# Turning the fourth batch's q and k by transposing transfers, spreading a bias by a matrix product, and a new order for the whole program

## The chip, the core and the metric

The kernel runs on one core of a Trainium2 chip. Five engines work side by side, each through its own list of instructions in order: PE (TensorE, matrix products; PEld is its loading of the stationary operand), DVE (VectorE), ACT (ScalarE), POOL (GpSimd) and SP (SyncE, which here only issues transfers). They wait for each other through semaphores. Transfers are issued from the lists of SP, ACT and POOL and are carried out by 16 DMA engines; SP's also do transposing transfers from SBUF to SBUF. The metric is the device time of one execution in microseconds (us), as a median over runs.

## What is computed

Cosine attention over 8 batches, 12 heads, 448 positions and a head dimension of 64, followed by a highway layer over all 3584 positions of width 768:

```python
q_n = q / (norm(q, axis=-1) + 1e-06)
k_n = k / (norm(k, axis=-1) + 1e-06)
scores = q_n @ k_n.T / tau                      # tau = 0.1
attn = softmax(scores)
x = (attn @ v), laid out as [8 * 448, 12 * 64]
H = maximum(x @ w_h, 0.0)
T = 1.0 / (1.0 + exp(-(x @ w_t + b_t)))
out = T * H + (1.0 - T) * x
```

## The kernel before

**Tiling.** Heads are worked on in pairs (head p and head p + 6), six pairs a batch, 48 steps s = 6 b + p in all. 448 positions are three chunks of 128 ("rows") and a tail of 64; the tails of a batch are handled together. Everything that goes into a matrix product is fp16; loads from DRAM convert on the way where POOL issues them.

**Stages of a batch b.** `load_main` and `load_v` (POOL's list) bring q, k, v rows into `qr`, `kr`, `vr`; `load_tails` (SP's list; for batch 0 k's on ACT's) brings the tails into `qt`, `kt`, `vt`. `square`, `tail_squares` and `folds` form the sums of squares (tile names `sq`, `f`, `n`), `newton` the reciprocal roots (`rs`). `scaled` multiplies rows by them into `qn`, `qtnorm` and `ktnorm` the tails into `kb`. Then q and k must be turned, the head dimension onto the partitions:

- `turn` (L565 on) and `turn_tails` (L594 on), for batches not in `BY_DMA`, on PE: seven 128x128 transposes a pair (L582 for six pieces of `qn`, L585 for the k tail in `kb`) into a PSUM tile `pB`, then one copy to `qT` on DVE or ACT (the line is that of the helper `copied`, L261); and three transposes of the batch's q tails (L607) with a copy to `tT` on DVE (L611).
- For batches in `BY_DMA`, `turn` issues one transposing transfer `qT<-qn` a pair (L572), and `turn_tails` one, `tT<-kb`, a batch (L599), both from SP's list.

`scores` makes the products of scores (L642 for the rows, four products a chunk on 64 rows of the array; L657 for the tail keys, on the whole array), each followed by an exponential on ACT (`E`, L648; `Et`, L661). `attend` multiplies by v on PE (L690, L694, L710; the appended column of ones in `vp` gives the sums) and DVE normalizes (`rd` L718, `x` L720). `ffn` takes a batch in four pieces g = 4 b + i: `x` is turned into `xT` (a transfer at L757 for batches 1 to 6, PE at L763 else), then products with `wt` and `wh` (L807 on 64 rows, L791 on 64 columns, L779 for the last piece), tanh on ACT (`tt`), and the gate on DVE and POOL (`hm` L867 and L879, `tt` L872, `os` L884), and stores from SP.

**The bias.** Up to piece 23 the bias enters as one more product: a row of ones times the bias, `pS<-bth,ones`, at the start of an accumulation. `bth` holds the bias in rows 0 and 64, zero elsewhere, loaded by two transfers (L375, POOL) after DVE has cleared it. From piece 24 (`ADDED`), that is from batch 6, DVE adds the bias from a tile `bias` that holds it on every partition (L837, L839). `bias` is filled by one broadcasting transfer from DRAM (L377, POOL).

**What sets the order.** The functions only write down 1717 operations, each with its engine and what it reads and writes. A table `ORDER` gives the order in which they are issued, and so the order of every engine's list; `SLOTS` says which buffer of its ring every tile gets (three PSUM tiles `pS` of two banks each, two `pB` of one, rings of two to four in SBUF); `MOVED` lists the operations that go to their second engine (`pick`); `URGENT` lists POOL operations that the next DVE operation must wait for. Nothing is decided at run time. At the start PE multiplies a constant tile with itself 40 times (`warm`, L310).

Of the kernel before, what the change touches and what calls it, by code (L numbers as in the profile page):

```python
# [20 lines left out]
18 17 2 3 5 0 78 20 19 33 83 21 6 23 11 4 84 24 29 22 77 1 16 8 74 87 28 75 42 25 36 81 40 9 43 27 26 35 32 44  # L21
278 45 31 46 276 7 47 30 56 48 49 274 51 57 50 13 54 34 55 58 10 59 65 52 60 94 76 61 99 72 273 14 53 62 98 100
63 64 95 117 488 90 118 101 82 93 487 91 105 66 489 103 106 107 92 277 96 104 67 119 275 68 137 120 281 136 15
490 69 279 97 108 138 283 122 70 71 300 38 139 128 280 175 129 39 145 194 86 146 12 193 126 37 491 89 156 127
109 174 88 1108 155 110 176 123 143 121 177 157 102 492 73 159 158 195 282 124 144 196 113 197 114 284 112 125
111 164 115 288 160 116 165 141 185 299 79 186 80 285 142 162 287 147 130 301 148 133 131 161 286 85 289 166
132 163 179 134 181 290 135 167 183 140 291 184 302 694 150 292 149 293 151 180 294 152 295 168 296 170 297 182
169 153 298 154 171 311 198 172 202 200 199 173 178 204 318 190 203 187 313 189 188 205 319 201 191 314 312 192
315 507 695 337 320 506 209 206 497 207 321 208 338 210 496 329 211 360 323 327 303 357 339 330 340 324 316 228
356 212 229 328 342 213 344 493 348 343 379 358 508 346 345 359 322 219 304 347 509 907 220 498 325 501 363 305  # L30
221 499 326 317 222 349 306 510 495 331 341 502 332 333 307 494 364 334 308 503 351 309 699 223 352 504 353 350
417 365 505 235 310 366 375 236 335 354 376 361 355 214 362 336 414 215 500 377 398 367 394 378 216 395 217 368
511 902 512 396 413 218 372 397 369 371 513 370 405 514 515 237 516 373 406 403 517 374 238 602 404 384 239 415
519 385 244 382 245 545 380 230 383 416 901 231 525 381 401 704 424 402 386 518 232 224 387 233 544 425 418 520
399 234 521 388 906 529 522 390 419 389 713 546 696 391 714 400 1109 246 392 547 526 393 697 420 247 225 905
422 421 527 601 408 703 528 407 582 409 410 698 603 548 423 564 532 604 248 533 411 553 563 412 249 554 583 536
428 226 427 537 429 426 250 555 430 620 251 431 556 534 523 252 432 535 715 530 260 584 531 705 549 903 253 261
585 524 551 716 565 700 552 706 539 566 540 538 550 1101 541 256 570 542 254 921 543 572 240 559 255 560 573
558 557 574 571 257 433 621 709 434 241 575 606 707 568 258 435 607 561 717 436 569 438 708 439 259 910 710 447
904 920 440 437 702 711 441 712 242 586 448 911 442 452 449 718 567 831 243 453 719 624 720 701 450 721 562 812  # L40
454 451 722 589 605 455 723 590 724 593 733 461 622 594 922 591 587 623 456 579 726 578 577 588 612 725 1102
262 613 752 265 592 443 1107 790 263 912 1110 266 576 727 728 264 267 608 580 916 610 581 751 462 1106 609 729
463 732 611 444 753 734 771 627 735 770 625 464 628 754 465 808 915 772 626 457 596 773 809 597 595 466 598 755
631 458 741 632 756 789 629 757 616 599 268 615 600 828 617 630 614 781 923 1302 476 782 445 742 479 917 477
924 1111 918 480 731 919 737 618 736 827 633 619 634 738 636 635 913 791 478 481 637 638 760 467 761 792 459
639 739 468 914 740 775 810 446 776 730 743 1301 469 811 460 744 758 269 470 908 759 270 762 1104 747 925 471
774 746 745 763 668 777 926 796 779 778 927 472 767 928 764 929 765 780 1112 748 654 977 1121 930 482 640 749
931 750 933 1120 655 766 1113 829 797 993 227 641 830 939 909 656 768 798 473 657 1105 799 957 642 769 995 643
658 938 645 644 956 940 646 1122 815 794 647 816 992 958 648 932 795 813 649 793 800 784 975 801 785 1103 786
814 783 483 994 838 484 836 839 834 659 1123 837 974 805 1303 804 787 1310 835 803 976 802 788 660 934 806 832  # L50
817 807 661 833 1029 935 662 818 474 819 663 843 1304 841 820 842 1114 840 1311 485 823 937 824 475 821 650 822
844 1320 1010 845 271 683 825 1136 686 826 1115 1011 1116 687 1124 846 684 1028 948 685 688 966 936 1030 946
651 669 947 1213 670 1321 1012 674 1117 1312 942 675 943 652 671 272 672 1306 1013 676 959 673 664 1305 677
1118 978 875 847 678 1505 979 848 679 960 1119 1511 852 486 1322 961 849 1323 1506 853 967 665 944 1315 850
1125 666 945 854 855 851 680 861 1126 856 941 862 949 1313 980 962 681 863 981 864 1127 1159 964 865 1128 951
1316 953 1002 1129 965 950 1130 952 1131 689 866 963 954 1324 1133 867 1003 982 1138 996 868 983 1139 869 955
# [116 lines left out]
def kernel(  # L173
# [11 lines left out]
    nc = tc.nc  # L185
# [824 lines left out]
```

## Time and profile before

| | us |
|---|---|
| median of 3 runs (lowest, highest) | 269.06 (268.74, 270.12) |
| the profiled execution, first to last instruction | 270.4 |
| busy: PE, DVE, ACT, POOL | 244.4, 228.5, 206.0, 115.9 |

The profile has no other time of the profiled execution than its span, and that lies 1.3 us over the median and 0.3 over the slowest run. Busy times are read with care: a PE product is shown from its start to a modelled end, and the products behind it start before that, so the starts tell how fast PE goes. Idle time in front of an instruction is put down to what ended it ("<-"). An answer cut into stretches gives the busy time of each engine in each; a share of DMA over 1 means that packets overlap.

### The profile page before, as it was taken

The numbers are of one execution on the slowest core, as the hardware profiler recorded it, in microseconds if no ns is written. First come the engines' busy times: TensorE is split into PE (matmuls) and PEld (weight loads), VectorE is DVE, ScalarE is ACT, GpSimd is POOL, SyncE is SP. The second block draws the span as 40 slices with busy tenths as digits, with TensorE's granted clock in tenths as the row PEclk, the third lists the DMA queues.
The fourth block names the chain that finished last, engine by engine and source line by source line (L and its number), as shares of the span: only waits on it lengthen the run. The fifth ranks groups of instructions, "written<-read, shape, count | busy, mean of one in ns | idle before, by whom it ended". The sixth has DMA issues, their size and how long they took to land.

```text
span 270.4 us, 9033 instructions
## 1 busy us (share of the span) xinstructions
PE 244.4 (90%) x3755; PEld 165.0 (61%) x3755; DVE 228.5 (85%) x513; ACT 206.0 (76%) x279; POOL 115.9 (43%) x151
## 2 busy tenths in 40 slices
PE   7088978999999999999899799997999999999991
PEld 3044666676776676667466557664767667767650
DVE  6599899999999898998976978997987864569894
ACT  3379999799999989989589499867868797961120
POOL 8757458563455649335450626314404522002140
PEclk9659999999999999999999799999999999999998
DMA  7999999999899797999999976999939949413133
GB/s 136 207 192 183 179 200 211 194 184 193 136 136 252 103 152 84 172 253 157 178 166 173 187 196 128 206 136 154 235 107 175 183 72 238 80 58 119 63 100 132
DMA packets 104025, 43.32 MB, mean 160 GB/s; under 512 B 97584, under 2 KB 101040, under 8 KB 103984
## 3 DMA queue, kind: packets, MB, share of 16 engines
q0 software_dynamic: 38608, 16.52, 49.1%
q1 hardware_dynamic: 63920, 25.50, 48.8%
q10 hardware_dynamic: 1456, 0.72, 1.0%
q8 instruction: 29, 0.48, 0.7%
q14 instruction: 12, 0.10, 0.1%
HBM read 38.21 MB, written 11.01 MB: 182 GB/s over the span
## 4 chain that ended last, share of the span: by engine, by line
PE 62%; DVE 20%; DMA 7%; issue 4%; ACT 3%; POOL 2%; SPq 1%; DVEq 0%; PEldq 0%; ACTq 0%; POOLq 0%
PE pS L807 26%; PE pS L642 9%; PE pB L694 8%; PE pS L791 4%; PE pB L710 4%; PE pB L657 3%; PE pB L690 3%; DMA kt<-in_k_dram 3%; DVE qn L258 3%; PE pB L582 2%; DMA qr<-in_q_dram 2%; DVE x L720 2%; DMA qT<-qn 2%; DVE f L421 2%; DVE hm L867 1%
## 5 line engine op out<-in xcount | busy, mean ns | idle before, releaser
L648 ACT ACTIVATE E<-pS 128x896 f16<-128x896 f32 x144 | 127.3, 924 | 26.2 <-PE pS L642 22.5
L807 PEld LDWEIGHTS <-xT 64*128 64x128 f16 x1128 | 53.8, 94 | 31.6 <-issue 2.6
L807 PE MATMUL pS<-wt,xT 64*128 64x384 f16 x576 | 56.6, 325 | 0.2 <-PEq L800 0.2
L807 PE MATMUL pS<-wh,xT 64*128 64x384 f16 x552 | 55.7, 323 | 0.2 <-DVE hm L867 0.2
L642 PE MATMUL pS<-qT 64*128 64x384 f16 x288 | 43.9, 332 | 2.3 <-DMA qT<-qn 1.8
L694 PE MATMUL pB<-vp,E 128*128 128x65 f16 x864 | 43.8, 194 | 0.0
L694 PEld LDWEIGHTS <-E 128*128 128x128 f16 x864 | 38.8, 98 | 2.6 <-issue 2.5
L867 DVE SCALAR_TENSOR_TENSOR hm<-pS,x 128x768 f16<-128x768 f32 (+1 forms) x33 | 27.3, 831 | 10.7 <-ACT tt L848 5.7
L642 PEld LDWEIGHTS <-qT 64*128 64x128 f16 x576 | 22.9, 95 | 19.6 <-issue 4.4
L690 PE MATMUL pB<-vp,Et 128*128 128x130 f16 x144 | 32.0, 222 | 2.3 <-DVE x L720 1.9
L258 POOL TENSOR_TENSOR qn<-kr,rs 128x384 f16<-128x384 f16 x24 | 19.8, 827 | 32.9 <-issue 10.0
L884 POOL TENSOR_TENSOR os<-x,hm 128x768 f32<-128x768 f16 (+1 forms) x11 | 15.8, 1441 | 37.7 <-DVE hm L879 17.3
L720 DVE SCALAR_TENSOR_TENSOR x<-pB,rd 128x448 f16<-128x448 f32 x48 | 29.7, 621 | 1.1
L661 ACT ACTIVATE Et<-pB 128x512 f16<-128x512 f32 x48 | 28.9, 609 | 0.9 <-PE pB L657 0.8
L642 PE MATMUL pS<-tT,qT 64*128 64x64 f16 x282 | 27.6, 190 | 0.0
L258 POOL TENSOR_TENSOR qn<-qr,rs 128x384 f16<-128x384 f16 x17 | 14.4, 850 | 14.0 <-DMA qT<-qn 5.6
L884 DVE TENSOR_TENSOR os<-x,hm 128x768 f32<-128x768 f16 (+1 forms) x22 | 18.5, 842 | 0.8 <-POOL os L884 0.6
L845 ACT ACTIVATE tt<-os 128x768 f16<-128x768 f32 (+1 forms) x8 | 6.1, 764 | 17.1 <-DVE os L839 10.0
L710 PE MATMUL pB<-vp,E 128*128 128x65 f16 x288 | 18.6, 195 | 0.5 <-POOL vp L261 0.5
L258 DVE TENSOR_TENSOR qn<-qr,rs 128x384 f16<-128x384 f16 x30 | 17.2, 577 | 0.5 <-POOL qn L258 0.4
L690 PEld LDWEIGHTS <-Et 128*128 128x128 f16 x144 | 14.1, 98 | 5.5 <-issue 4.3
L879 DVE TENSOR_TENSOR hm<-tt,hm 128x768 f16<-128x768 f16 (+1 forms) x33 | 16.4, 503 | 0.4
(116 smaller groups left out, 451.2 us busy)
## 6 DMA issues: line engine op xcount, KB each, us to landing
out_dram<-os SPq DMA_DIRECT2D x23, 384.0 KB, 3.0
vr<-in_v_dram POOLq DMA_DIRECT2D x8, 576.0 KB, 11.3
kr<-in_k_dram POOLq DMA_DIRECT2D x7, 576.0 KB, 10.8
qr<-in_q_dram POOLq DMA_DIRECT2D x7, 576.0 KB, 10.7
qt<-in_q_dram SPq DMA_DIRECT2D x16, 96.0 KB, 5.4
vt<-in_v_dram SPq DMA_DIRECT2D x16, 96.0 KB, 5.6
out_dram<-os SPq DMA_DIRECT2D x15, 96.0 KB, 2.7
kt<-in_k_dram SPq DMA_DIRECT2D x14, 96.0 KB, 6.7
```

The costliest lines, as they stand in the source:

```text
L258: return (nc.vector if eng == "DVE" else nc.gpsimd).tensor_mul(out_, a, c)
L642: ins = nc.tensor.matmul(dst, lhsT=qT[ln, 384 + 128 * c : 512 + 128 * c], rhs=rhs, start=True, stop=True)
L648: return nc.scalar.activation(R("E", s)[:, c, :, 0:448], R("S", 3 * s + c)[:, :, 0:448], AF.Exp, scale=inv_tau)
L661: op("ACT", f"expt {s}", lambda: nc.scalar.activation(R("Et", s)[:, 64:576], R("B", ("S", s))[:, :], AF.Exp, scale=inv_tau), key + 3, r=[( ...
L690: nc.tensor.matmul(U[:, 2 * c : 2 * c + 2, :].rearrange("p g e -> p (g e)"), lhsT=Et[:, 128 + 128 * c : 256 + 128 * c], rhs=vp[:, 6:8, :]. ...
L694: ins = nc.tensor.matmul(U[:, 2 * c + ab, :], lhsT=EF[:, j, 576 * ab + 128 * c : 576 * ab + 128 * c + 128], rhs=vp[:, 3 * ab + j, :], star ...
L710: ins = nc.tensor.matmul(U[:, 6, :], lhsT=lt, rhs=rh, start=(n == 0), stop=(n == 7))
L720: op("DVE", f"ev {s}", lambda: nc.vector.scalar_tensor_tensor(out=R("x", b)[:, :, D * p : D * p + D], in0=U_()[:, :, 0:D], scalar=0.0, in1 ...
L807: ins = nc.tensor.matmul(P[:, h, 0:MH], lhsT=lt, rhs=rh, start=(part == 0 and cc == (-1 if wi == 0 and not added else 0)), stop=(part == 1 ...
L867: return nc.vector.scalar_tensor_tensor(out=o_, in0=i0, scalar=0.0, in1=xs, op0=ALU.max, op1=ALU.subtract)
L879: op("DVE", f"gg{'h' if tail or last_ else ''} {nm}", lambda cs=cs: nc.vector.tensor_mul(R("hm", g)[:, cs], R("tt", g)[:, cs], R("hm", g)[ ...
L884: op(en, f"out{'h' if tail or last_ else ''} {nm}", lambda eng=eng, cs=cs: eng.tensor_add(R("os", g)[:, cs], xall()[:, cs], R("hm", g)[:, ...
```

## The change

Four things change together.

1. `BY_DMA` takes in batch 3. Its six turns on PE with their six copies, and the turn of its tails with a copy, become seven transposing transfers in SP's list.
2. The bias tile is no longer loaded by a broadcast. Two products `pS<-bth,ones` (`spread`, L380 of the new file) put the bias on all partitions of a PSUM tile, and one copy brings it to `bias`, on DVE or ACT; `MOVED` puts it on ACT.
3. `ORDER`, `SLOTS`, `MOVED` and `URGENT` are new from the first entry to the last. 104 operations change between DVE and POOL (54 to POOL, 50 to DVE), 25 between DVE and ACT (12 to ACT, 13 to DVE), 7 between ACT and POOL. `URGENT` has 37 entries in place of 50.
4. There are 1711 operations in place of 1717.

```diff
-18 17 2 3 5 0 78 20 19 33 83 21 6 23 11 4 84 24 29 22 77 1 16 8 74 87 28 75 42 25 36 81 40 9 43 27 26 35 32 44
...
+21 18 6 16 27 40 26 17 8 20 29 25 24 19 1 44 0 39 43 3 5 4 2 45 46 47 48 49 50 7 51 54 28 55 52 53 56 22 23 32
...
-    BY_DMA = (4, 5, 6, 7)
+    BY_DMA = (3, 4, 5, 6, 7)
...
-        op("POOL", "ld bb", lambda: nc.gpsimd.dma_start(bias[:, :], moe_b_t.partition_broadcast(128)), key + 30, w=[("bias", 0)])
+
+        def spread():
+            for h in range(2):
+                ln = slice(64 * h, 64 * h + 64)
+                ins = nc.tensor.matmul(R("S", ("bb", 0))[:, h, 0:MH], lhsT=ones[ln, 0:128], rhs=bth[ln, MH * h : MH * h + MH],
+                                       start=True, stop=True)
+            return ins
+
+        op("PE", "bbm", spread, key + 30, mode="T", r=[("zb", 0), ("bth", 0)], w=[("S", ("bb", 0))])
+        eng = pick("DVE", "ACT")
+        op(eng, "bbc", lambda eng=eng: copied(eng, bias.rearrange("p (h m) -> p h m", h=2), R("S", ("bb", 0))[:, :, 0:MH]), key + 30,
+           r=[("S", ("bb", 0))], w=[("bias", 0)])
```

Lines of the new file are one lower than the old ones up to L374, and ten higher behind the bias.

Three places of the new order. The first is ACT at the start of the program, before (`first` is the first pair's rows, `first_sq`, `first_n` and `first_rs` its squares, sums and roots; a number behind a name is the buffer):

```order
L264 ACTIVATE sq_89<-qt_76 128x384
L264 ACTIVATE sq_89<-qr_70 128x2x2x192
L264 ACTIVATE sq_90<-kr_73 128x2x3x192
L454 ACTIVATE rs_98<-n_96,tiny 128x36
L456 ACTIVATE rs_98<-rs_98 128x36
L264 ACTIVATE sq_90<-qr_70 128x2x3x192
L261 COPY qT_105<-pB_135 128x896
L648 ACTIVATE E_108<-pS_131 128x2x448
```

and now:

```order
L263 ACTIVATE sq_89<-qr_71 128x2x2x192
L263 ACTIVATE sq_89<-qt_77 128x384
L263 ACTIVATE sq_89<-kt_79 128x384
L260 COPY qT_106<-pB_134 128x896
L260 CAST bias<-pS_133 128x768
L464 ACTIVATE rs_100<-n_96,tiny 128x36
L466 ACTIVATE rs_100<-rs_100 128x36
L263 ACTIVATE sq_89<-kr_75 128x2x3x192
L263 ACTIVATE sq_89<-qr_71 128x2x3x192
L671 ACTIVATE Et_112<-pB_134 128x512
L658 ACTIVATE E_110<-pS_131 128x2x448
```

The first turn's copy has moved ahead of the roots and of the squares of pairs 3 to 5; the square of a k tail and the copy of the bias are new on ACT here.

The second is DVE at the start, from the sum of the first pair's squares to the copy of its turned q tail (`first_kb` is its k tail, `first_qtn` its q tail), before:

```order
L502 TENSOR_REDUCE first_n<-first_fb 128x15
L258 TENSOR_TENSOR sq_89<-kr_73 128x2x2x192
L506 TENSOR_TENSOR qn_101<-first,first_rs 128x2x3x64 x2
L516 TENSOR_TENSOR first_kb<-first_t,first_rs 64x64
L258 TENSOR_TENSOR sq_89<-kt_78 128x384
L421 TENSOR_TENSOR f_92<-sq_89 128x1152
L511 TENSOR_TENSOR first_qtn<-first_t,first_rs 128x128
L425 TENSOR_TENSOR f_94<-f_92 128x576
L427 TENSOR_REDUCE n_96<-f_94 128x36
L281 MEMSET Et_112 128x32 x2
L516 TENSOR_TENSOR first_kb<-first_t,first_rs 64x64
```

and now:

```order
L512 TENSOR_REDUCE first_n<-first_fb 128x15
L280 MEMSET first_kb 64x32 x2
L516 TENSOR_TENSOR qn_102<-first,first_rs 128x2x3x64
L526 TENSOR_TENSOR first_kb<-first_t,first_rs 64x64 x2
L516 TENSOR_TENSOR qn_102<-first,first_rs 128x2x3x64
L521 TENSOR_TENSOR first_qtn<-first_t,first_rs 128x128
L257 TENSOR_TENSOR sq_89<-kr_75 128x2x2x192
L431 TENSOR_TENSOR f_92<-sq_89 128x1152
```

Both halves of `first_kb`, on which the first turn waits, now stand right beside `qn`, ahead of the squares and folds of the next pairs. PE's list begins with one pair of `warm` products, then the two products `pS<-bth,ones`, four pairs of `warm` products and the first turn; before it began with eight pairs of `warm` products and the turn of `first_qtn`. In POOL's list the two loads of `bth` are now the second and the fifth transfer; before, the fourth and one behind the large loads of the first batches.

The third is SP around the fourth batch's transfers, before:

```order
L757 DMA_TRANSPOSE xT_119<-x_117 128x9x128
L361 DMA kt_79<-in_k_dram 64x6x64
L757 DMA_TRANSPOSE xT_120<-x_118 128x12x128
L898 DMA out_dram<-os_130 128x768
L898 DMA out_dram<-os_128 128x768
L367 DMA vt_86<-in_v_dram 64x6x64
L357 DMA qt_77<-in_q_dram 64x6x64
L757 DMA_TRANSPOSE xT_119<-x_118 128x9x128
```

and now:

```order
L908 DMA out_dram<-os_128 128x768
L582 DMA_TRANSPOSE qT_105<-qn_101 128x6x128
L366 DMA vt_86<-in_v_dram 64x6x64
L767 DMA_TRANSPOSE xT_120<-x_117 128x9x128
L582 DMA_TRANSPOSE qT_105<-qn_101 128x6x128
L908 DMA out_dram<-os_129 128x768
L360 DMA kt_79<-in_k_dram 64x6x64
L609 DMA_TRANSPOSE tT_104<-kb_80 128x9x128
L582 DMA_TRANSPOSE qT_106<-qn_102 128x6x128 x2
L356 DMA qt_77<-in_q_dram 64x6x64
L767 DMA_TRANSPOSE xT_119<-x_118 128x12x128
```

The transfers `qT<-qn` and `tT<-kb` of batch 3 stand among loads and stores of other batches; the load of half of k's tails of batch 4 (`kt_79` here) stands behind three transposing transfers. Its square was on ACT and is now on DVE.

## What the change will do to the time

> **What bounds the kernel now.** I read the page's shares first, then the span cut at the places where its character changes (stretches in us).
>
> ```profile
> PE 244.4 (90%) x3755; PEld 165.0 (61%) x3755; DVE 228.5 (85%) x513; ACT 206.0 (76%) x279; POOL 115.9 (43%) x151
> ```
>
> ```profile
> 18.00:50.00 32.00, 27.04 (x430) 18.57 (x425) 30.44 (x68) 31.06 (x43) 18.99 (x29) 0.98 1.36 193
> 50.00:130.00 80.00, 79.35 (x1312) 55.46 (x1310) 74.65 (x171) 73.59 (x99) 42.54 (x50) 1.00 1.17 167
> 130.00:246.00 116.00, 111.18 (x1789) 75.31 (x1784) 91.36 (x199) 90.14 (x122) 34.78 (x45) 0.99 0.89 157
> 246.00:270.40 24.40, 18.00 (x208) 11.35 (x204) 19.19 (x37) 3.58 (x5) 5.49 (x4) 0.96 0.28 98
> ```
>
> After each stretch stand its length and the busy us of PE, PEld, DVE, ACT and POOL, then the granted clock and the DMA share. There are four regimes. From 18 to 50 ACT has 31.06 of 32 us, DVE 30.44, and PE is not the limit. From 50 to 130 PE has 79.35 of 80: what is taken from it there counts in full. From 130 to 246 PE stands still for 116.00 - 111.18 = 4.8 us. The last stretch is PE's last matrix products and the output. What ends PE's long waits is in the view of waits (total us, times, longest), with one link of the chain of work.
>
> ```profile
> DVE sq L258 <- DMA kt<-in_k_dram: 2.3, 1, 2.3
> PE pB L690 <- DVE x L720: 1.9, 1, 1.9
> PE pS L642 <- DMA qT<-qn: 1.8, 1, 1.8
> PE pB L657 <- DMA tT<-kb: 1.1, 1, 1.1
> 138.36 8.51 DMA kt<-in_k_dram
> ```
>
> All three waits of PE begin with a transfer that landed late: two are transposing transfers, and the one of 1.9 came through DVE, which had waited 2.3 us for k's tail rows of batch 6, 8.51 us under way. They sum to the 4.8. The two stretches beside the 1.9 one show what else it may have cost:
>
> ```profile
> 148.70:152.10 3.40, 1.51 (x40) 1.42 (x39) 3.40 (x7) 0.95 (x3) 1.43 (x2) 1.00 1.46 195
> 152.20:155.50 3.30, 3.30 (x40) 2.22 (x39) 3.27 (x8) 2.20 (x3) 2.76 (x4) 0.50 1.33 179
> 185.10:188.80 3.70, 1.94 (x26) 0.95 (x23) 2.47 (x7) 2.94 (x5) 0.53 (x1) 1.00 0.90 154
> 188.90:192.20 3.30, 3.30 (x76) 2.69 (x76) 3.08 (x7) 2.15 (x3) 2.74 (x5) 1.00 1.56 269
> ```
>
> Behind PE's half-idle 3.4 us the granted clock is 0.50 for 3.3 us, worth half of that, 1.65 us. Behind the like wait for qT at 188.8 it stays at 1.00.
>
> **The change part by part.** First PE's transposes of the fourth batch: they go. The timeline around two of its turns, and a change of the array's mode:
>
> ```profile
> 95.59 0.51 PE L582 MATMUL pB<-ident,qn 128*128 128x128 f16 x6
> 95.94 0.22 PE L585 MATMUL pB<-ident,kb 128*128 128x128 f16 x1
> 95.99 0.50 PE L582 MATMUL pB<-ident,qn 128*128 128x128 f16 x6
> ...
> 99.35 0.19 PE L657 MATMUL pB<-tT,qT 128*128 128x64 f16 x1
> 99.38 0.33 PE L657 MATMUL pB<-qT 128*128 128x384 f16 x1
> 99.55 0.19 PE L657 MATMUL pB<-tT,qT 128*128 128x64 f16 x1
> 99.67 0.34 PE L642 MATMUL pS<-qT 64*128 64x384 f16 x2
> ```
>
> Starts are what counts, since the ends overlap. One turn is 95.99 - 95.59 = 0.40 us for seven, so six turns are 2.40 and the three transposes of the tails 3 x 0.40/7 = 0.17: **-2.57 us**, in the stretch where PE is full. Against it: a 64-column product at 99.35 is followed 0.03 later by one of the same mode, at 99.55 one of another mode follows 0.12 later, so a change costs 0.09. I count the neighbours of different mode (64 rows in L642 and L807, 64 columns in L791, the whole array elsewhere) in PE's list: 135 before, 153 now. 18 x 0.09 = **+1.62 us**. This new order interleaves products of two kinds more finely, and it eats most of what the transposes gave.
>
> The copies behind the turns go too, and the bias gets its product, and a copy on ACT (bias<-pS). The prices:
>
> ```profile
> L261 DVE COPY qT<-pB 128x896 f16<-128x896 f16 x16 | 9.8, 617 | 0.9 <-PE pB L585 0.6
> L261 ACT COPY qT<-pB 128x896 f16<-128x896 f16 x8 | 7.3, 914 | 1.0 <-PE pB L585 1.0
> L849 ACT ACTIVATE tt<-pS 128x768 f16<-128x768 f32 x18 | 14.6, 820 | 1.4 <-PE pS L807 1.3
> L264 ACT ACTIVATE sq<-kt 128x384 f16<-128x384 f32 x4 | 2.2, 546 | 0.0
> ```
>
> The six copies of batch 3 stood on DVE: 6 x 0.62 = 3.7 us less there. PE is full in that stretch and hardly waits for DVE, so this counts as nothing directly; it is slack for later. If PE's cover were gone there, it would be worth up to those 3.7.
>
> **The start.** These rows lead up to the first exponential:
>
> ```profile
> 13.91 0.29 PE L618 MATMUL pB<-ident,first_qtn 128*128 128x128 f16 x1 [7.82 <-DVE first_qtn L511]
> 13.99 1.48 PE L310 MATMUL pB<-fill 128*128 128x384 f16 x4
> 15.01 0.18 DVE L516 TENSOR_TENSOR first_kb<-first_t,first_rs 64x64 f16<-64x64 f32 x1
> 15.28 0.84 PE L582 MATMUL pB<-ident,qn 128*128 128x128 f16 x6
> 15.54 1.15 ACT L264 ACTIVATE sq<-qr 128x1152 f16<-128x1152 f16 x1
> 16.59 0.88 ACT L261 COPY qT<-pB 128x896 f16<-128x896 f16 x1
> 17.53 0.50 PE L642 MATMUL pS<-qT 64*128 64x384 f16 x2
> 18.13 1.73 ACT L648 ACTIVATE E<-pS 128x896 f16<-128x896 f32 x2 [0.65 <-PE pS L642]
> ```
>
> The first turn waited for the second half of first_kb, which DVE reached only at 15.01; now both halves follow qn at once, some 4 us earlier. But ACT still has both squares of pairs 3 to 5 ahead of its first exponential, the later one from 15.54 to 16.69 (its input is not loaded earlier), and the bias copy besides (0.82, by the tanh over 128x768 from PSUM, the nearest row). So the first exponential can come at 16.7 + 0.8 = 17.5 at best, 0.6 earlier. Up to the end of batch 0 ACT gets one square of a tail (0.55), the bias copy (0.82) and one turn copy net (0.91) more, 2.3 us; at batch 2's squares one like the 1.15 row and one of a tail (0.55) go back to DVE, and +0.6 is left, against the 0.6 gained: **0**, bounds -0.6 and +1.7 (all 2.3 kept, less 0.6).
>
> **The transfers.** Seven transposing ones come onto SP's queue; the broadcast of the bias leaves POOL's.
>
> ```profile
> qT<-qn SPq DMA_TRANSPOSE x24, 3.6
> tT<-kb SPq DMA_TRANSPOSE x4, 4.7
> bias<-in_moe_b_t_dram POOLq DMA_DIRECT2D x1, 192.0 KB, 9.2
> ```
>
> In four batches, 28 such transfers made PE wait 1.8 + 1.1 = 2.9 us, 0.7 a batch: **+0.7** for the batch that is new, bounds 0 (each is issued long enough before its product) and 2.9. Behind a transfer that waits for its qn, SP holds the loads and stores that come next. The lost broadcast counts 0: its 9.2 us were hidden, since the added bias is used only from batch 6 on.
>
> **The rest of the order.** The 1.9 us wait and the 1.65 of clock came from one collision: k's tail of batch 6 against three large loads. The order is new everywhere, and DVE has 3.7 us less to do before that place. I take half of 3.55 as gone, **-1.8**, because a new order will have places of its own; bounds -3.55 and 0.
>
> The Trainium skill, page "TensorE: Matmul & The Clock Gate", Part 1, says that the clock halves after at least one idle window of about 3.4 us. The rows here do not agree: PE was busy for 1.51 of the 3.40 us ahead of the halving. By the page the halving would not be the wait's doing, and the -1.8 would be half of 1.9 alone, -0.95.
>
> Sum: -2.57 + 1.62 + 0 + 0.7 - 1.8 = -2.05 us. The profiled execution spans 270.4, 1.3 over the median of the three runs; I carry the difference to the median: 269.06 - 2.05 = **267.0 us**. A measurement of this kernel can tell about 0.5%, 1.35 us, from no change.
>
> **The rivals.**
> - *The waits stay.* The new order has its 3.55 us elsewhere: -2.57 + 1.62 + 0.7 = -0.25, 268.8. For it: the late landings are not in the order's hands. Against: DVE is lighter. 0.20.
> - *The halving has another cause* than the wait: then it is left as it is, half of 1.9 goes, and the sum is -1.2, 267.9. For it: the wait at 188.8 was not followed by one. Against: the halving at 152.2 stands right behind the other. 0.05.
> - *All waits of PE for transfers go*, 2.9 and 3.55: -2.57 + 1.62 - 2.9 - 3.55 = -7.4, 261.7. For it: the loads have been laid out afresh. Against: seven transfers more. 0.10.
> - *Slower: the bias product holds PE up at the start.* It stands second in PE's list, behind one pair of warm-up products, and waits for both rows of the bias:
>
> ```profile
> L375 POOL DMA_DIRECT2D bth<-in_moe_b_t_dram x2: 516/532/547, 4.9 to 22.7; - x2
> DMA to landing us min/median/max: 5.0/13.2/21.5
> ```
>
> The load issued at 4.9 took 5.0 us, the other, issued at 22.7 among large loads, 21.5. Now both are issued among the first six of POOL, by about 5 us (4.9 is where such a place was). Landing 5.0 later, they let PE go at 10. Behind them come four pairs of warm-ups (0.74 a pair by the 1.48 for two, 3.0 in all), the turn (0.84) and its copy (0.88), 4.7 us. So it costs from a landing at 17.5 - 4.7 = 12.8 on, one for one; with the median of 13.2 us it lands at 18.1, +5.3, and the time is 272.3. 0.10.
> - *Slower: a second collision.* The second half of k's tail for batch 4 now stands on SP behind three transposing transfers, and its square has moved from ACT to DVE, as the one at batch 6 did its harm. One more 3.55 with the old one kept: -2.57 + 1.62 + 0.7 + 3.55 = +3.3, 272.4. It decides if the load lands more than about 2 us after DVE reaches the square. 0.13.
>
> **How the numbers follow.** The forecast has 0.42. Faster by over 0.5%: 0.42 + 0.10 = 0.52; within: 0.20 + 0.05 = 0.25; slower: 0.10 + 0.13 = 0.23. The bounds of the terms alone give -2.57 + 1.62 + 0 - 3.55 - 0.6 = -5.1 (264.0) to -2.57 + 1.62 + 2.9 + 0 + 1.7 = +3.65 (272.7). The upper end takes in both slower rivals; the lower goes to 263.0, part of the way to the case of 0.10 below. The forecast's own range is 265.2 to 267.7.
>
> **What would show it.** PE: 45 transposes fewer in L592, L595 and L617 of the new file, 153 changes of mode. Waits: how much of PE's idle time past 50 us is ended by qT, tT, xT or a load, against 4.8 + 1.65 now. Start: the second PE group at 10 us, the first exponential near 17.5. The clock: a stretch at 0.50 past 30 us only behind a wait of over 1.5 us. I am wrong if PE's busy time past 50 us does not fall by about 1 us, if the first product comes later than 17.5, or if a single wait of more than 2 us stands in the new trace.

## The result and the profile after

| | before | after |
|---|---|---|
| median, us (lowest, highest) | 269.1 (268.7, 270.1) | 285.1 (283.6, 288.9) |
| ratio, 95% interval | 1 | 1.0555 (1.047 to 1.064) |
| profiled execution, span | 270.4 | 281.8 |

The kernel is 5.6% slower; the forecast was 267.0, and no rival went past 272.4. The profiled execution of the new kernel took 283.6 us, its fastest of four, so the profiles differ by 11.4 us where the medians differ by 16; what fills the other 4.6 us is in no profile. Three of the profiles below (pool_behind_kb, pe_turns_new_order, bias_loads) are of executions 2 to 4% longer than the fastest of the same kernel, while the ratios compare the faster ones (only two each for pool_behind_kb and pe_turns_pool_apart); what such a profile alone shows is not used as a cause.

The page of the new kernel, its shares, the granted clock in 40 slices of 7.0 us, and the engines on the chain of work that ended last:

```profile
PE 245.7 (87%) x3712; PEld 161.2 (57%) x3712; DVE 228.2 (81%) x504; ACT 208.2 (74%) x282; POOL 122.3 (43%) x150
PEclk9999986999999999599999999999999999999998
PE 45%; DVE 20%; DMA 16%; issue 6%; POOL 5%; SPq 4%; ACT 2%; DVEq 0%; POOLq 0%; PEldq 0%; ACTq 0%
```

Before, PE had 62% of that chain and DMA 7%. The clock has two dents, at 41 to 47 and at 112 to 119 us. The stretches around them, one from 60 to 74 us, and the last three of the prediction's four (length, then the busy us of PE, PEld, DVE, ACT, POOL, then the clock and the DMA share):

```profile
30.00:38.80 8.80, 6.29 (x131) 4.68 (x128) 8.56 (x21) 8.20 (x11) 4.99 (x7) 1.00 1.39 183
38.80:43.00 4.20, 0.03 (x2) 0.05 (x1) 4.12 (x6) 1.46 (x3) 2.42 (x4) 0.72 1.16 213
43.00:47.40 4.40, 4.35 (x42) 3.13 (x43) 2.29 (x6) 3.68 (x5) 2.99 (x5) 0.50 1.16 210
60.00:74.00 14.00, 11.45 (x173) 7.10 (x170) 12.16 (x25) 13.16 (x17) 10.72 (x14) 1.00 1.13 127
110.10:113.40 3.30, 0.23 (x4) 0.01 (x2) 2.37 (x5) 1.13 (x3) 1.31 (x2) 0.84 1.61 160
113.40:119.10 5.70, 5.70 (x77) 4.45 (x78) 1.53 (x4) 3.67 (x5) 2.15 (x3) 0.50 1.36 161
...
50.00:130.00 80.00, 73.88 (x1133) 48.97 (x1132) 68.19 (x150) 66.25 (x88) 41.89 (x48) 0.96 1.16 157
130.00:246.00 116.00, 111.49 (x1800) 73.56 (x1797) 92.28 (x202) 95.92 (x133) 42.11 (x48) 1.00 1.02 170
246.00:281.80 35.80, 30.20 (x411) 19.10 (x408) 26.74 (x52) 10.74 (x14) 7.48 (x5) 0.97 0.26 90
```

Twice PE stands still for 3.3 to 4.2 us and then runs at half clock for 4.4 and 5.7: 4.2 + 2.2 and 3.3 + 2.85, 12.5 us in all. From 60 to 74, where PE had been full, it has 11.45 of 14. The view of waits names what PE waited for (five of its rows):

```profile
PE pB L667 <- DVE x L730: 5.1, 2, 4.2
PE pS L380 <- DMA bth<-in_moe_b_t_dram: 4.2, 1, 4.2
PE pS L652 <- DMA tT<-kb: 3.1, 1, 3.1
PE pS L817 <- DMA xT<-x: 2.8, 3, 1.6
PE pB L592 <- DVE tT L621: 1.6, 1, 1.6
```

The second is the bias product's, at the start, where PE has nothing else to do. The others are losses. How far PE is behind over the program tells when: I count the 3492 recorded products of scores, values and weights (the bias rows among them), and give the time at which a share of them had ended (us).

| done | before | after | three_repairs | loads_apart | both_old_order |
|---|---|---|---|---|---|
| 5% | 35.7 | 37.8 | 37.6 | 37.3 | 35.2 |
| 10% | 50.5 | 56.5 | 51.7 | 51.4 | 50.0 |
| 20% | 75.3 | 85.0 | 78.3 | 78.0 | 74.8 |
| 30% | 100.7 | 108.9 | 102.6 | 101.8 | 105.4 |
| 35% | 112.0 | 124.0 | 112.0 | 111.3 | 116.9 |
| 40% | 123.5 | 135.4 | 131.5 | 122.6 | 133.4 |
| 60% | 170.6 | 181.6 | 176.7 | 173.4 | 176.3 |
| 100% | 264.4 | 276.4 | 270.3 | 267.6 | 268.0 |

The new kernel is 2.2 us behind at 5% of its products, 9.7 at 20%, 12.0 at 35%, and 12.0 at the end: what comes behind 35% costs nothing more. The three columns on the right are experiments, below.

**The wait at 43 us.** DVE's timeline up to the eviction `x` (it takes the finished sums out of the PSUM buffer and so frees it), and POOL's beside it (start, length in us):

```profile
36.67 0.75 DVE L437 TENSOR_REDUCE n<-f 128x36 f32<-128x576 f16 x1
37.46 3.02 DVE L475 TENSOR_SCALAR rs<-n 128x36 int32<-128x36 int32 x1
40.49 1.73 DVE L257 TENSOR_TENSOR kb<-kt,rs 64x384 f16<-64x384 f32 x2
42.15 0.19 DVE L728 RECIPROCAL rd<-pB 128x7 f32<-128x7 f32 x1
42.38 0.62 DVE L730 SCALAR_TENSOR_TENSOR x<-pB,rd 128x448 f16<-128x448 f32 x1
```

```profile
37.28 1.07 POOL L364 DMA_DIRECT2D vr<-in_v_dram  x1
38.37 0.84 POOL L257 TENSOR_TENSOR qn<-qr,rs 128x384 f16<-128x384 f16 x1
39.17 0.83 POOL L257 TENSOR_TENSOR qn<-kr,rs 128x384 f16<-128x384 f16 x1
39.94 0.50 POOL L260 COPY vp<-vr 128x384 f16<-128x384 f16 x1
40.40 0.82 POOL L257 TENSOR_TENSOR qn<-qr,rs 128x384 f16<-128x384 f16 x1
```

An operation on 36 numbers a partition counts as busy for 3.02 us, and ends only when POOL has issued the load and been through three operations in a row (39.94 + 0.50 = 40.44). DVE was not working, it was held. It was no wait that the program orders: the only semaphore that this instruction waits for is DVE's own, and `n` had set it by 37.44. What let it go is open, since a fourth operation of POOL follows at 40.40 without a gap. The same happens once more, at 69.73, as POOL is issuing a load (68.86 to 69.87) with another row of four behind it that ends at 72.4:

```profile
69.73 3.10 DVE L257 TENSOR_TENSOR qn<-kr,rs 128x384 f16<-128x384 f16 x1
```

**The wait at 113 us.** The chain of work (start, us, what):

```profile
104.78 8.56 DMA tT<-kb
113.39 0.61 PE pS L652 x6
```

The transfer of the fourth batch's `kb` was issued 5.2 us before PE needed it and took 8.56 us. Two large loads on POOL, of 576 KB each, had been issued at 104.52 and 106.77 and landed at 114.03 and 119.68.

### The profile page after: what moved, and what is told of

It reads as the page before. It is cut to its first block, busy times and chain, and to the rows that moved or that the text cites. A ratio compares the mean times of both kernels' runs of the same rounds, so it can differ in the third digit from the quotient of the medians.

```text
span 281.8 us, 8947 instructions
## 1 busy us (share of the span) xinstructions
PE 245.7 (87%) x3712; PEld 161.2 (57%) x3712; DVE 228.2 (81%) x504; ACT 208.2 (74%) x282; POOL 122.3 (43%) x150
## 4 chain that ended last, share of the span: by engine, by line
PE 45%; DVE 20%; DMA 16%; issue 6%; POOL 5%; SPq 4%; ACT 2%; DVEq 0%; POOLq 0%; PEldq 0%; ACTq 0%
PE pS L817 20%; PE pS L652 6%; PE pB L704 6%; DMA tT<-kb 5%; DMA kt<-in_k_dram 3%; PE pS L801 3%; DVE qn L257 3%; DMA qT<-qn 3%; DVE x L730 3%; PE pB L720 3%; PE pB L667 3%; PE pB L700 2%; DMA kr<-in_k_dram 2%; DVE n L437 2%; DVE hm L877 2%
## 5 line engine op out<-in xcount | busy, mean ns | idle before, releaser
L817 PEld LDWEIGHTS <-xT 64*128 64x128 f16 x1128 | 48.3, 94 | 38.0 <-PEq L810 4.6
L817 PE MATMUL pS<-wt,xT 64*128 64x384 f16 x576 | 60.2, 323 | 2.9 <-DMA xT<-x 2.8
L817 PE MATMUL pS<-wh,xT 64*128 64x384 f16 x552 | 58.6, 324 | 0.0
L652 PE MATMUL pS<-qT 64*128 64x384 f16 x288 | 46.2, 331 | 2.4 <-DMA qT<-qn 1.3
L704 PE MATMUL pB<-vp,E 128*128 128x65 f16 x864 | 45.4, 197 | 1.3 <-DVE vp L260 1.3
L894 POOL TENSOR_TENSOR os<-x,hm 128x768 f32<-128x768 f16 (+1 forms) x14 | 20.2, 1446 | 47.6 <-DVE hm L889 28.3
L257 POOL TENSOR_TENSOR qn<-qr,rs 128x384 f16<-128x384 f16 x25 | 21.3, 859 | 26.4 <-DVE qn L257 6.3
L728 DVE RECIPROCAL rd<-pB 128x7 f32<-128x7 f32 x48 | 9.5, 199 | 15.3 <-PE pB L720 6.9
L859 ACT ACTIVATE tt<-pS 128x768 f16<-128x768 f32 x18 | 14.7, 819 | 5.4 <-PE pS L817 3.9
L257 DVE TENSOR_TENSOR qn<-kr,rs 128x384 f16<-128x384 f16 x26 | 16.9, 654 | 2.2 <-POOL os L894 1.8
L720 PE MATMUL pB<-vp,E 128*128 128x65 f16 x288 | 18.6, 196 | 0.0
```

The costliest lines, as they stand in the source:

```text
L257: return (nc.vector if eng == "DVE" else nc.gpsimd).tensor_mul(out_, a, c)
L652: ins = nc.tensor.matmul(dst, lhsT=qT[ln, 384 + 128 * c : 512 + 128 * c], rhs=rhs, start=True, stop=True)
L704: ins = nc.tensor.matmul(U[:, 2 * c + ab, :], lhsT=EF[:, j, 576 * ab + 128 * c : 576 * ab + 128 * c + 128], rhs=vp[:, 3 * ab + j, :], star ...
L720: ins = nc.tensor.matmul(U[:, 6, :], lhsT=lt, rhs=rh, start=(n == 0), stop=(n == 7))
L817: ins = nc.tensor.matmul(P[:, h, 0:MH], lhsT=lt, rhs=rh, start=(part == 0 and cc == (-1 if wi == 0 and not added else 0)), stop=(part == 1 ...
L859: return nc.scalar.activation(T.rearrange("p (h m) -> p h m", h=2), P[:, :, 0:MH], AF.Tanh, scale=0.5)
```

## The experiments

All edits are to the order tables; the code changes only where an experiment takes a part of the change alone. In the diffs stand rows of an engine's list. "Measured" is the ratio to the kernel before, run beside the experiment, with its 95% interval. The fourth batch is batch 3 in the code's counting from 0. In the first three, theory A is that the new order does the harm, theory B that the parts of the change do; from there on each expectation says what its theories are.

**One part, or both, in the order of before.** bias_old_order has the code of the bias product, and both loads of `bth` early on POOL; batch4_old_order has `BY_DMA = (3, 4, 5, 6, 7)`, and on SP

```diff
 L756 DMA_TRANSPOSE xT_119<-x_117 128x9x128
+L598 DMA_TRANSPOSE tT_104<-kb_81 128x9x128
+L571 DMA_TRANSPOSE qT_105<-qn_102 128x6x128 x2
 L360 DMA kt_79<-in_k_dram 64x6x64
+L571 DMA_TRANSPOSE qT_107<-qn_101 128x6x128
+L571 DMA_TRANSPOSE qT_106<-qn_102 128x6x128
+L571 DMA_TRANSPOSE qT_107<-qn_101 128x6x128
+L571 DMA_TRANSPOSE qT_106<-qn_102 128x6x128
 L756 DMA_TRANSPOSE xT_120<-x_118 128x12x128
```

> The order of before, with one part of the change: the bias spread by the TensorE product (it stands in PE's 7.82 us of idle time ahead of the first turn, its copy on ACT behind the square of a tail) in place of the DRAM broadcast. Theory A, the loss comes from places in the new order: 0, 269.1 (within 0.5%), since both lie in idle time and the broadcast was hidden. Theory B, the parts of the change cost by themselves: the product at the start would put off the first score product and the time goes to 272 or more.

Measured: 0.9964 (0.992 to 1.001). The bias part costs nothing.

> The order of before, with the other part of the change: q and k of the fourth batch turned by seven transposing transfers on SP, each placed as soon as its normed inputs are there; 45 transposes of PE and seven copies of DVE are gone. Theory A: -2.57 for the transposes, up to 1 us back where a transfer lands later than the old turn was ready, so 266.5 to 268.0. Theory B: the transposing transfers of this batch land late in any order, PE waits 3 us and runs at half clock behind it for some 6 us, as it does at 113 us in the new kernel: 274 or more.

Measured: 1.036 (1.030 to 1.042).

> The order of before with both parts. Theory A: the sum of the two runs with one part, 266.5 to 268.5, faster than before, so the new order alone turned a gain of 1 to 2 us into a loss of 16. Theory B: 275 to 285, most of the loss is there without the new order.

Measured: 1.028 (1.0225 to 1.033). Theory A falls in this form. PE's waits in batch4_old_order, and the stretch of the longer one with the one behind it:

```profile
PE pS L641 <- DMA qT<-qn: 6.0, 2, 5.7
PE pS L806 <- DMA xT<-x: 5.0, 1, 5.0
```

```profile
98.60:104.30 5.70, 0.05 (x2) 0.00 (x0) 3.08 (x8) 0.94 (x2) 0.00 (x0) 0.74 1.38 193
104.30:108.20 3.90, 3.87 (x48) 2.68 (x50) 0.00 (x0) 1.96 (x3) 3.29 (x4) 0.50 0.42 82
```

The fourth batch's transfers land late in the old order too: three of them, issued from 94.0 to 98.1, landed at 102.8 to 104.3, just behind a load of `vr` issued at 91.75 that landed at 102.37. So the parts of the change do harm by themselves; but the table has both_old_order 0.5 us ahead at 20%, where the new kernel is 9.7 behind, so the new order does harm of its own.

**The transfer of `kb` earlier on SP.**

```diff
 L767 DMA_TRANSPOSE xT_120<-x_117 128x9x128
+L609 DMA_TRANSPOSE tT_104<-kb_80 128x9x128
 L582 DMA_TRANSPOSE qT_105<-qn_101 128x6x128
 L908 DMA out_dram<-os_129 128x768
 L360 DMA kt_79<-in_k_dram 64x6x64
-L609 DMA_TRANSPOSE tT_104<-kb_80 128x9x128
```

> The new kernel with one move on SP's queue: the transposing transfer of the tails and k of batch 3 (tT from kb) goes ahead of a transfer of qn, a store and a load of kt, some 3 us earlier and ahead of the two large loads on POOL at 104.5 and 106.8. Theory A: the wait of 3.25 us at 113 us goes, and with it the stretch at half clock behind it (6.1 us busy at 0.50, worth 3.0): 285.1 - 6.2 = 279, ratio to before about 1.036, no idle time of PE over 1 us between 100 and 120 and a granted clock of 1.00 there. Theory B: the transfer lands as late as it did, or the wait passes to the transfer that now stands behind it: 284 to 286. A third reading, that the half clock has nothing to do with the wait: the wait goes and the half clock stays, 282.

Measured: 1.091 (1.085 to 1.097), slower still, which none of the three expected. The transfer did land 4.0 us after its issue and not 8.6. But the load of `kt` behind it (k's tail rows of the fifth batch) was now issued 1.2 us after the load of `vr` and not 0.5 before it, and took 9.1 us where it had taken 3.6. DVE's timeline:

```profile
114.84 0.56 DVE L257 TENSOR_TENSOR sq<-kt 128x384 f16<-128x384 f32 x1 [8.53 <-DMA kt<-in_k_dram]
```

DVE stood for 8.53 us with the evictions and gates queued behind, and PE for 6.6. Later in this trace a transfer of `xT`, issued at 148.8 between two large loads, took 11.9 us, and PE waited 6.0 for it. The late landing goes to whichever transfer stands behind the load.

**The large loads later, SP as it was.**

```diff
 L257 TENSOR_TENSOR qn_102<-kr_75,rs_100 128x2x3x64
-L364 DMA vr_84<-in_v_dram 128x12x192
 L257 TENSOR_TENSOR qn_101<-kr_75,rs_100 128x2x3x64
-L341 DMA kr_75<-in_k_dram 128x12x192
 L435 TENSOR_TENSOR f_95<-f_92 128x192
+L364 DMA vr_84<-in_v_dram 128x12x192
+L341 DMA kr_75<-in_k_dram 128x12x192
```

> The new kernel with the repair of the wait at 113 us alone, from the other side: the two large loads on POOL (vr of batch 5, kr of batch 6; first used some 30 us later) go behind the next operation of POOL, from 104.5 and 106.8 to about 110 or later. The queue on SP stays as it is. Theory A, a transfer that is issued with a large load in flight lands only when that load does: tT, issued at 104.8, lands by 108.5 and not at 113.3, the two of qn behind it within 4 us and not 10, kt of batch 4 stays early; the wait of 3.25 and the half clock behind it (3.0) go: 279, ratio about 1.035. Theory B, it lands late because of the queue on SP or of the transposing itself: 284 to 286.

Measured: 1.055 (1.049 to 1.061), no gain. From issue to landing the transfer of `kb` takes, in the new kernel and then in this one:

```profile
DMA to landing us min/median/max: 8.6/8.6/8.6
```

```profile
DMA to landing us min/median/max: 3.2/3.2/3.2
```

Theory A was right about this transfer and not about the total: the loads went out at 113.1 and 114.2, the transfer of `xT` at 115.7 stood behind them, took 10.6 us, and PE waited 3.6 for it and ran 4.9 us at half clock. The same loss, 13 us later.

**POOL's row of operations apart from DVE's.** In the table of the order, four operations of POOL go behind the two products `kb` of DVE, which makes them wait for these; and one eviction on DVE goes ahead:

```diff
+L728 RECIPROCAL rd_114<-pB_135 128x7
+L730 SCALAR_TENSOR_TENSOR x_116<-pB_135,rd_114 128x7x64
 L478 TENSOR_TENSOR rs_99<-rs_99 128x36
-L728 RECIPROCAL rd_114<-pB_135 128x7
-L730 SCALAR_TENSOR_TENSOR x_116<-pB_135,rd_114 128x7x64
```

> The new kernel with the repair of the wait at 43 us alone: four operations of POOL (qn and kn of pair 6, a copy of v, qn of pair 7) go behind the two products kb of batch 1 on DVE, and one eviction of DVE (rd and x of pair 2) ahead of the second step of the Newton iteration. Nothing else moves. Theory A, DVE's small operation at 37.46 took 3.02 us because POOL ran four operations back to back beside it, and the eviction that PE waited for stood behind it: the operation takes 0.2 to 0.4, PE's idle 4.23 us ahead of L667 shrinks to under 1, the clock stays at 1.00 from 42 to 48, and 4.23 - 0.7 + 2.2 = 5.7 us go: 279.4, ratio to before about 1.035. Theory B, DVE waits there for something else (the load on POOL that is issued at 37.28 writes its descriptors): the operation stays at about 1 us or more, and 282 or more is left. Theory C, the half clock does not hang on the wait: 281.5.

Measured: 1.037 (1.031 to 1.044), theory A to the point. The load at 37.3 is still there; DVE's timeline:

```profile
37.51 0.18 DVE L475 TENSOR_SCALAR rs<-n 128x36 int32<-128x36 int32 x1
37.70 1.14 DVE L257 TENSOR_TENSOR kb<-kt,rs 64x384 f16<-64x384 f32 x2
38.77 0.19 DVE L728 RECIPROCAL rd<-pB 128x7 f32<-128x7 f32 x1
38.99 0.62 DVE L730 SCALAR_TENSOR_TENSOR x<-pB,rd 128x448 f16<-128x448 f32 x1
```

The held operation takes 0.18 and not 3.02, PE's wait is under 1 us, and the clock stays at 1.00. both_repairs, below, has the same edit, and its shorter execution shows the same. Its DVE timeline and the stretch around it:

```profile
37.31 0.18 DVE L475 TENSOR_SCALAR rs<-n 128x36 int32<-128x36 int32 x1
40.33 0.88 DVE L257 TENSOR_TENSOR sq<-kt 128x384 f16<-128x384 f32 x1
```

```profile
38.00:46.00 8.00, 6.47 (x118) 4.84 (x116) 6.45 (x16) 7.93 (x10) 7.17 (x11) 1.00 1.17 211
```

POOL's row now runs from 38.73 on, seven operations without a gap, and `sq` beside it takes 0.88 us where 0.55 is usual: a row alone held DVE for 0.33. The load alone did not hold it: POOL issues it from 37.14 to 38.21, and the operation at 37.31 passes. In all 17 traces ten operations of DVE took over 2 us more than their like, and each began while POOL was issuing a load with a row right behind; without that pair none took over 1.2 us more. So the long holds come with the pair; the experiments moved the row, and no run moved the load.

The Trainium skill ("SBUF — State Buffer", "SBUF: two separate sides") has DVE, in some of its operations, and GpSimd share a port pair that whichever starts first holds for its whole instruction. The trace agrees that one blocks the other, but the hold went on over three operations of POOL, none over 0.84 us.

**Both repairs, and more of the kind.** both_repairs joins the last two. three_repairs makes four POOL operations at 65 us wait for `qn` of pair 12 on DVE, and puts the two loads behind three more POOL operations. loads_apart puts `kr` back in its place, and `vr` behind the next load of `qr`:

```diff
 L257 TENSOR_TENSOR qn_101<-kr_75,rs_100 128x2x3x64
+L341 DMA kr_75<-in_k_dram 128x12x192
 L435 TENSOR_TENSOR f_95<-f_92 128x192
-L364 DMA vr_84<-in_v_dram 128x12x192
-L341 DMA kr_75<-in_k_dram 128x12x192
...
 L341 DMA qr_71<-in_q_dram 128x12x192
+L364 DMA vr_84<-in_v_dram 128x12x192
```

> The new kernel with both repairs. If the two waits are separate, their gains add: 285.1 - 5.7 - 6.1 = 273.3, ratio about 1.014, and what is left over before is spread over smaller waits (a turn at 74 us 1.8, xT at 151 us 1.75). If the later part of the order sets its own pace (the loads and DVE's work behind 120 us), the second gain is lost again before the end: 278 to 280.

Measured: 1.040 (1.034 to 1.047). The gains do not add: the loads stand ahead of `xT` once more, and PE waits 3.5 us for it.

> The new kernel with both repairs and two more steps of the same kind: at 65 us four operations of POOL that ran back to back (two copies of v, qn of pairs 17 and 16) wait until DVE has done qn of pair 12, and the two large loads of 107 us go two operations further back on POOL, behind the output of token block 5, so that they are issued after the transfer of xT and not ahead of it. Theory A (DVE is held while POOL runs back to back; a transfer issued behind large loads waits for them): kn of pair 13 on DVE takes 0.6 and not 3.09 us, the wait of 1.6 us for the turn of pair 13 goes; xT lands within 4 us and not 10.5, the wait of 3.5 us at 120 us and the half clock behind it (3.7 busy us at 0.50, 1.9) go. 281.2 - 1.6 - 3.5 - 1.9 = 274.2, ratio about 1.015. If the transfers behind xT now stand in for it (two of qn, issued by 118): 277 or more.

Measured: 1.033 (1.027 to 1.039).

> The new kernel with the two repairs of POOL's operations beside DVE's (at 37 and 65 us), the load kr of batch 6 in its own place, right behind kn of pair 23, and the load vr of batch 5 behind that of qr of batch 6, from 108.5 to about 118 us. In three_repairs PE was 0.7 us behind the kernel before at 35% of its work and then waited 5.6 us for a transfer of qn that was issued at 114.0 with both loads in flight, with 3.1 busy us at half clock behind it. Theory A (transfers issued behind large loads wait for them): that wait and the half clock go, 280.3 - 5.6 - 1.5 = 273, ratio about 1.01. If the next transfers, of xT and qn issued from 119 on with two loads in flight, stand in for it: 277 or more.

Measured: 1.0185 (1.010 to 1.027). In three_repairs the second held operation and, in the next two fences, the longest wait of PE there and in loads_apart:

```profile
64.92 0.55 DVE L257 TENSOR_TENSOR qn<-kr,rs 128x384 f16<-128x384 f16 x1
```

```profile
PE pS L652 <- DMA qT<-qn: 6.3, 2, 5.6
```

```profile
PE pB L667 <- DMA tT<-kb: 4.8, 2, 4.5
```

`qn` takes 0.55 and not 3.10, and at 35% of its products three_repairs is level with before. Then it waits 5.6 us for a transfer behind the loads: the case that its expectation had at 277 or more. loads_apart takes that away, is 0.8 us ahead of before at 40%, and meets the next one, the fifth batch's `tT`, 4.5 us with 3.4 us at half clock behind it. That one loss, 4.5 + 1.7 = 6.2 us, is more than the 1.85% (5.0 us) by which it is slower than before.

**The fourth batch back on PE, in the new order.** The turns stand up to 3 us behind where the transfers stood; the second run also has POOL's operations apart.

```diff
-    BY_DMA = (3, 4, 5, 6, 7)
+    BY_DMA = (4, 5, 6, 7)
```

> The new order with the part on the fourth batch undone: its q and k are turned by PE again (45 transposes and seven copies of DVE, placed where the transfers stood or up to 3 us behind), the bias product stays. With the two runs of the old order this fills the table of old or new order by PE or transfers. Theory A, both cost and at different places: the wait for tT at 113 us and its half clock go (3.25 + 3.0), the transposes come back (2.57), the hold of DVE at 37 and 65 us stays (5.7 + 1.6): 285.1 - 6.25 + 2.6 = 281.5, ratio about 1.045. Theory B, the transfers are the whole loss: 269 to 271. Theory C, the order is the whole loss: 285 or more.

Measured: 1.077 (1.065 to 1.089).

> The same, and the two repairs of POOL's operations beside DVE's (those of pool_behind_kb, and the four operations at 65 us behind qn of pair 12). Theory A: 281.5 - 5.7 - 1.6 = 274, ratio about 1.018; what is left over before would be the finer mixing of the new order and its other waits. If the holds of DVE and the transfers are all of it: 270 to 272. Theory B: as the run before.

Measured: 1.036 (1.027 to 1.046). The difference of 4% shows the holds of DVE once more. What the new order costs without the transfers can't be read from these two: beside the turns, between 97 and 121 us of the second run, PE has seven new waits of 0.7 to 1.5 us. They probably come from where the turns were put, with two buffers `pB` to share; no run tried other places.

**The rule in the order of before.** both_old_order_loads moves three loads of both_old_order:

```diff
 L894 TENSOR_TENSOR os_128<-x_116,hm_126 128x768
+L342 DMA kr_75<-in_k_dram 128x12x192
 L894 TENSOR_TENSOR os_129<-x_116,hm_125 128x768
 L261 COPY vp_88<-vr_83 128x6x64
 L258 TENSOR_TENSOR kb_81<-kt_79,rs_98 64x6x64
-L342 DMA kr_75<-in_k_dram 128x12x192
 L365 DMA vr_84<-in_v_dram 128x12x192
...
+L258 TENSOR_TENSOR kb_80<-kt_78,rs_99 64x6x64
 L342 DMA qr_70<-in_q_dram 128x12x192
-L258 TENSOR_TENSOR kb_80<-kt_78,rs_99 64x6x64
```

> The order of before with both parts, and three large loads on POOL moved out of the way of the transposing transfers: kr of batch 5 from 90.0 to about 82, vr of batch 5 from 91.0 to about 87, qr of batch 6 from 112.5 to behind the product kb. Theory A (large loads in flight put off the transfers): tT and the first two of qn of the fourth batch land by 101 and not at 102 to 104, xT of 112.8 well before 121; of the waits of 5.8 and 3.8 us and the half clock behind them at least half goes, 277.3 to about 270, ratio 0.995 to 1.01. Theory B: they land as late as they did, 276 or more.

Measured: 1.016 (1.012 to 1.021). The loss falls from 2.8 to 1.6%, short of the 0.995 to 1.01 of theory A. PE no longer waits for the transfers of `qn`, but `xT`, issued at 87.6 among the loads that had been moved, took 12.1 us and held PE for 5.1.

one_load_earlier is the kernel before with one load moved:

```diff
 L425 TENSOR_TENSOR f_95<-f_93 128x576
+L342 DMA qr_70<-in_q_dram 128x12x192
 L884 TENSOR_TENSOR os_128<-x_117,hm_126 128x768
-L342 DMA qr_70<-in_q_dram 128x12x192
```

> The kernel before with one instruction moved: the large load on POOL (qr of batch 6) ahead of the output operation that stood before it, 1.6 us earlier, from 108.2 to 106.6, and so ahead of the transfer of xT that is issued on SP at 107.4. Theory A, a transfer that finds two large loads in flight waits for them: xT lands at about 115 and not at 111.95, PE waits 2 to 3 us for it at 113, and the clock halves behind it; 269.1 + 2.5 + 1.5 = 273, ratio about 1.015. Theory B, a landing depends on the amount under way, not on who is issued first: within 0.5% of before.

Measured: 1.0044 (1.0004 to 1.008). The transfer of `xT` takes 4.5 us in before and here 8.9:

```profile
DMA to landing us min/median/max: 4.5/4.5/4.5
```

```profile
DMA to landing us min/median/max: 8.9/8.9/8.9
```

```profile
113.40:116.00 2.60, 0.00 (x1) 0.00 (x0) 2.43 (x9) 2.54 (x3) 0.86 (x2) 0.77 1.19 244
116.00:121.60 5.60, 5.57 (x42) 2.92 (x44) 0.85 (x3) 0.00 (x0) 0.79 (x1) 0.50 0.96 257
```

The place costs more than was expected, 2.6 + 2.8 = 5.4 us against 4, but the total is theory B's, within 0.5% of before. At the end 1.5 us are left in the span (271.9 against 270.4), and the waits of before at 150 and 188 us are no longer there; presumably, with PE late at 116, what they waited for had landed.

bias_loads and bias_loads_2 start from bias_old_order. The first moves `qr` of batch 6 behind `kb`, the second also two of the three loads at 140 us:

```diff
+L258 TENSOR_TENSOR kb_80<-kt_78,rs_99 64x6x64
 L342 DMA qr_70<-in_q_dram 128x12x192
-L258 TENSOR_TENSOR kb_80<-kt_78,rs_99 64x6x64
...
 L342 DMA qr_71<-in_q_dram 128x12x192
+L258 TENSOR_TENSOR kb_81<-kt_79,rs_100 64x6x64
 L365 DMA vr_83<-in_v_dram 128x12x192
 L342 DMA kr_74<-in_k_dram 128x12x192
```

> The order of before with the bias product, and one large load on POOL (qr of batch 6) moved behind the next operation, from 107.8 to about 114 us, after the transfer of xT that was issued at 107.1 and landed at 115.3. Theory A: xT lands by 111, PE's wait of 2.1 us and the half clock behind it (2.8 busy us at 0.50, 1.4) go: 268.35 - 3.5 = 264.9, ratio about 0.984, faster than before. The risk is that the transposing transfers of batch 5, issued from 122 on, now find the load in flight: then 267 to 269.

Measured: 0.994 (0.990 to 0.997), 0.6% faster than before where 1.6% were expected: `xT` landed 4.4 us after its issue and PE did not wait for it. bias_old_order, without the moved load, has 0.9964, inside this interval, so what the move alone is worth can't be told. Where the other 1% went is open: the profile, of a longer execution, has k's tail of batch 6 land late (DVE 3.3 us, PE 2.9).

> bias_loads with two more large loads moved: vr and kr of batch 7 on POOL go behind the product kb of batch 5, from 141 and 142 to about 150 us. In bias_loads k's tail rows of batch 6 were issued on SP between the three loads and landed 8.7 us later; DVE waited 3.3 us for them, PE 2.9 behind that, and 3.2 busy us ran at half clock. Theory A: k's tail lands by 146, DVE's wait and PE's go: 269.25 - 2.9 - 1.6 = 264.8, ratio 0.98 to 0.985, the best of all versions. Theory B, the wait comes back at the transfers of qn and kb at 154 to 156: 268 to 269.

Measured: 1.008 (1.003 to 1.012). Theory B, and worse: k's tail came in time, and the wait went on to the transfer of `kb`, 2.7 us at 156.

## Why the prediction was wrong, point by point

Two terms of the sum failed. "The transfers", +0.7 with 2.9 as the worst, had the right mechanism and the wrong size: in the old order the fourth batch's transfers cost 2.8 to 3.6%, 7.5 to 9.7 us, with the gain of the transposes already taken off. "The rest of the order", -1.8 with 0 as the worst, had the wrong sign: the new order put PE 9.7 us behind in the first fifth of its products, ahead of any transfer of the fourth batch.

- *The transposes and the changes of mode* (-2.57 and +1.62). PE has 43 instructions less, 45 transposes out and two products in. The size can't be read from the busy times, since the clock differs in the first 20 us. loads_apart, without a long wait there, gains 3.6 us on the kernel before between 20 and 40% of the products (2.7 behind, then 0.8 ahead); that fits the -2.57 and shows nothing of the +1.62, but the order differs there too. PE's time past 50 us did not fall by 1 us, it rose from 208.5 to 215.6, with 2.85 of half clock and with work in it that had stood before 50 us: by its own test the forecast was wrong there. So it was by another, a single wait of over 2 us: there are two, of 4.2 and 3.1.
- *The copies* (0, slack). The slack was there and bought nothing.
- *The start* (0; -0.6 to +1.7). ACT's first exponential starts at 17.41, as worked out (17.5), the first product of scores at 14.74 and not 17.53:

```profile
17.41 0.58 ACT L671 ACTIVATE Et<-pB 128x512 f16<-128x512 f32 x1
```

```profile
14.74 0.34 PE L652 MATMUL pS<-qT 64*128 64x384 f16 x2
```

  But at 5% of the products the kernel is 2.2 us behind, 0.5 past the bound: from 26 to 36 us PE waits three times, 0.9 to 1.3 us each.
- *The bias* (0, and as a rival 272.3 from a landing at 12.8 on). Both rows landed by 9.3 us, so the rival's own condition was not met; bias_old_order shows no cost.
- *The transfers* (+0.7, bounds 0 and 2.9). The mechanism was right, the size was not. 0.7 was an average over four batches, most of whose transfers had been issued with no large load in flight. I sorted the transposing transfers past 60 us by how many 576 KB loads were in flight at their issue: 7 of 40 had one or two in before, 16 of 47 in after. At 113 us it cost 3.3 + 2.85 us locally and 3.8 net (8.2 behind at 30%, 12.0 at 35%), past the bound of 2.9.
- *The rest of the order* (-1.8; bounds -3.55 and 0). "A new order will have places of its own" was priced as half of the old places, with 0 as the worst: new places worse than the old ones were left out. The wait at 150.8 and its half clock did go, and a wait for `xT` of 1.6 stands at 151. But the new order put PE 9.7 us behind by 20% of the work, and three_repairs, which puts the rows of POOL operations apart from DVE's, gets 6.7 of it back. No step and no rival had an engine held by another one; the page of the profile shows it only as busy time.
- *The rivals.* "A second collision", 0.13, had the right sign and kind. It named k's tail of the fifth batch behind the transposing transfers: in the new kernel that load got away by 0.5 us, and in tT_earlier it did what the rival said, at 8.5 us of DVE's time and not the 3.55 that a repeat of the old wait would cost.
- *The half clock.* That it is the wait's doing was right: each of the 26 stretches below full clock between 30 and 250 us, in the 17 traces, stands behind 3.4 us in which PE was busy for at most 1.8 (1.51 in the prediction's row), and where a repair took the wait, it took the half clock. The wait at 188.8, on which the rival leaned, does not speak against it. In each trace the stretches begin and end on one grid of 3.41 us; on that of before, the window of this wait has 1.66 us of PE, and the 13 windows of all traces with 1.44 to 1.79 at full clock went either way, seven into half clock and six not.

Not settled: what the new order costs with neither holds nor transfers; the single waits of about 1 us between 26 and 36 us were not tried.

## What to carry to other kernels

Before work is moved from an engine to a transfer, look at where each new transfer would stand among the large loads: here one lands 3.7 us after its issue behind none, 6.3 behind one and 9.2 behind two, and taking one out of the way can hand the late landing to the next in the queue. When an order is made anew, look for a load issued by GpSimd with a row of its operations right behind, beside VectorE's work; a small VectorE operation that shows a busy time of many times its like was not working here but held. A gain worked out for one stage needs a price for the waits that the new order may make, and that price has no zero as its worst end.

## What the runs showed of the hardware

- *Landing by loads in flight.* Over 750 transposing transfers of all the traces past 60 us, the median from issue to landing was 3.7 us with no 576 KB load in flight (522 of them), 6.3 with one (181) and 9.2 with two or more (47). Plain loads and stores from SP behave alike: stores of `os` had medians of 2.7, 5.6 and 7.2, and `kt` took 3.6 and 9.1 us on the two sides of one load.
- *DVE held by POOL.* 3.02 and 3.10 us for operations of 0.2 and 0.55, while POOL issued a load and went through three and four operations right behind it; with the row put behind DVE's operations, 0.18 and 0.55. A row without a load cost 0.33 (0.88 for 0.55), a load without a row nothing.
- *The half clock comes in steps.* Its stretches last 3.4 or 6.8 us (once 10.2), on one grid of 3.41 us a trace. Of 1008 windows of these grids between 30 and 245 us, all with less than 1.44 us of PE at full clock were followed by half clock, and none with over 1.79. The Trainium skill ("TensorE: Matmul & The Clock Gate", Part 1) has a free-running window of about 3.4 us, which agrees, and asks for an idle window, which does not: up to 1.79 busy us of 3.41 were no protection.
- *A load issued 1.6 us sooner* put off another queue's transfer by 4.4 us.
